# Copying x inside DRAM in 5 KB pieces, and three dummy products that read a constant of the preamble

## The chip, the cores and the metric

The kernel runs on one core of one Trainium2 chip. The metric is the device time of one execution in microseconds (us); smaller is better. Three runs of the kernel before gave 662.64, 663.84 and 665.05 us, so its median is 663.84 us.

## The reference

The kernel computes one transformer layer with its two branches in parallel, for a sequence of 2048 rows of width 640 in bf16. Cut to what matters:

```python
B, S, D, H = 1, 2048, 640, 32          # Dh = 20; F = 1536
xn = _layernorm(x)                     # per row
q = (xn @ wq).reshape(B, S, H, Dh)     # 32 heads of queries
k = xn @ wk                            # ONE head of keys, shared by all
v = xn @ wv                            # ONE head of values
p = softmax(q @ k.T * Dh ** -0.5)      # 32 x 2048 x 2048 scores
A = (p @ v) @ wo
h = relu(xn @ w1 + b1)
B = (h * h) @ w2 + b2
return x + A + B
```

## The kernel before

**Stages.** The rows of x are loaded in 16 tiles of 128 rows (`X0` to `X12`, L622, on the queues of SyncE and ScalarE). Each tile is normalised: `bn_stats` and `bn_aggr` on VectorE (L662 to L664) or two activations on ScalarE (L657, L658), a reciprocal root on ScalarE (first four tiles) or as a power on GpSimd (`PW4` to `PW15`, L676), and the product (`XN..`, L677) on VectorE or GpSimd. TensorE transposes the tile (`T..`, L700), VectorE or ScalarE evacuates it into `xnT` (`TE..`, L694, L696). From `xnT` come the keys (`K..`, `KT..`), the queries (`Q0_..`, `Q1`, `QC..`) and the values (`V..`, L703).

**The long middle.** For 32 blocks of 512 query rows by 4 heads, TensorE makes score tiles of 128 keys by 512 queries (`q:` and `d:` in the order). ScalarE takes the exponential of two of them at a time (L1083); part of the tiles goes to VectorE (L1093), GpSimd (L1106) and accumulating transfers instead, which build the exponential from four shifted copies in 16-bit arithmetic. TensorE then multiplies by the values (`v:`, `u:`). The feed-forward branch (`FFN..`, `FP..`, `OUT..`) and the query projections of later blocks are woven in between. L600 is the one line of nearly all matmuls.

**The order.** Each engine follows a list written out by hand (`ORDER`), in program order. An operation waits by semaphores for what it depends on; if it waits, everything behind it on its engine waits too. Three stretches of these lists matter here.

- TensorE begins with `W4 W5 W6`, three 128x512 dummy products into banks 4, 5 and 6 (L710), then thirteen more (`warm:`, L1041). Seven of those wait for nothing but the two constants, six for steps of the row statistics. Then come `T0 T1 T2 T3 K0 Q0_0 ...`. Later stands `q:38,39 q:40,41 Q1 Q1 T12 Q1 T13 q:42,43 Q1 q:44,45 Q1 KT6`.
- GpSimd runs `... PW11 XN11 PW12 XA PW13 PW14 XN14 PW15 XN15 LIB` and then the shifted copies.
- SyncE issues `X0 X2 wq0 X4 X6 X8 b2 X12 xb b1 w11 wq w10 w20 w22 w23 w13 QD2_2 ...`. Some of these hold until a named step: `xb` and `wq` wait for `TE2`, `b1` for `TE5`.

**The steps that the change touches.** `W4 W5 W6` multiply `ones_bf` (128x128) by `hT_tmp[:, 0, :]` (128x512 zeros). Both are set by VectorE (`ones`, L604, and `zero`, L605), and the three products wait for them. `xb` is a copy of x from its input in DRAM to a scratch tensor in DRAM (L647), 2560 KB, whose two sides are written as 128 rows of 20 KB. GpSimd's `XA` (L648) waits for it, and adds the bias b2 to it in DRAM; from there `XR..` (L869) fetches x + b2 tile by tile, from 53 us on, for the residual (L890, L900). `wq` (L628) brings the query weights apart from the first 80 columns; `Q1` (L773) and all `QC..` need it. `BC..` (L969) spreads the reciprocals of the softmax sums over the rows of the heads: its source has the heads as outermost dimension, one to four of them.

```python
nc.const_aps.tensor(1.0, (128, n), BF16)   # in the changed kernel: a bf16 constant of one column,
                                           # set by GpSimd before the engines start, read as n columns
```

Of the kernel before, what the change touches and what calls it, by code (L numbers as in the profile page):

```python
# [7 lines left out]
BF16 = mybir.dt.bfloat16  # L8
# [30 lines left out]
def _pl(z):  # L39
# [20 lines left out]
HOLD = dict(wq="TE2", b1="TE5", w1=("TE4", "TE6", "TE8", "TE10"), w2=("TE12", "TE13", "TE14", "TE15"), wo=("RL3_2", "RL3_4"), wd="RL3_7",  # L60
            fr=[f"OUT{16 + k}.16" for k in range(4)])
# [433 lines left out]
def bass_parallel_sum__grouped_kv_mqa__dense_activation_squared_relu__prompt_kernel(nc, A_x, A_wq, A_wk, A_wv, A_wo, B_x, B_w1, B_b1, B_w2, B_b2, out):  # L495
    es = ExitStack()
    with es:
        def sb(name, shape, dt):
            return es.enter_context(nc.sbuf_tensor(name, list(shape), dt))
# [28 lines left out]
        ones_bf = OR[:, 1, 0:64].bitcast(BF16)  # L528
# [7 lines left out]
        hT_tmp = sb("hT_tmp", [128, 2, 512], BF16)  # L536
# [8 lines left out]
        ps = es.enter_context(nc.psum_tensor("ps", [128, 8, 512], F32))  # L545
# [23 lines left out]
        xb = nc.dram_tensor("xb", [S, D], BF16, kind="Internal").ap()  # L569
# [14 lines left out]
        def one():  # L584
            nsem[0] += 1
            return newctr(f"d{nsem[0]}")
# [3 lines left out]
        def op(name, eng, fn, deps=(), **kw):  # L590
            o = Op(name, eng, fn if isinstance(fn, list) else [fn], deps, **kw)
            assert name not in made, name
            made[name] = o
            return o

        def load(name, eng, fn, deps=()):
            return op(name, eng, fn, deps, dma=one())
# [6 lines left out]
        c_ones = op("ones", "DVE", lambda e: e.memset(ones_bf[:], 1.0))  # L604
        c_zero = op("zero", "DVE", lambda e: e.memset(hT_tmp[:, 0, :], 0.0))  # L605
# [38 lines left out]
            lambda e: e.dma_start(wd32[:, DH:32, 1, :], hrows(wr0)[:, 8:DH, :])))]  # L644
        op("texp", "ACT", lambda e: e.preload_act_table_set("natural_log_exp_and_others"))
        l_b2 = load("b2", "SP", lambda e: e.dma_start(b2r[0].rearrange("(a n) -> a n", a=ST), B_b2.rearrange("(o n) -> o n", o=1).to_broadcast([ST, D])))
        l_xb = load("xb", "SP", lambda e: e.dma_start(xb.rearrange("(p a) d -> p (a d)", p=128), A_x[0].rearrange("(p a) d -> p (a d)", p=128)), [HOLD["wq"]])  # L647
        xa_op = op("XA", "POOL", lambda e: e.dma_start(xb.rearrange("(p a) d -> p (a d)", p=128).rearrange("p (k n) -> p k n", k=5),  # L648
                                                       b2r.rearrange("o (k n) -> o k n", k=5).to_broadcast([128, 5, 2048]), accum_op=ALU.add, max_dma_last_dim=4096), [l_b2, l_xb], dma=one())

# [55 lines left out]

        VB0, WB = SHARED[2], 7
        k_of, q_of, v_of, vs_of, first_rel = {}, {b: [] for b in range(NBLK)}, {}, {}, {}
        for bk in SHARED:
            op(f"W{bk}", "PE", lambda e, bk=bk: e.matmul(ps[:, bk, :], ones_bf[:, :], hT_tmp[:, 0, :], start=True, stop=True), [c_ones, c_zero])  # L710
        vmm = []
        for st in range(4):
            cs = slice(128 * st, 128 * st + 128)
# [316 lines left out]
        for e in ENG:  # L1030
            nth = {}
            for word in ORDER[e].split():
                w, _, ns = word.partition("@")
                ns = [int(x) for x in ns.split(",")] if ns else []
                k, _, a = w.partition(":")
# [52 lines left out]
        for _, a, e, ns in planned("e"):  # L1088
            u, hs = int(a.split(".")[0]), [int(h) for h in a.split(".")[1]]
            x = sets.setdefault(u, Terms())  # L1090
            i, n = len(x.order), len(hs)
# [8 lines left out]
        for u, x in sets.items():  # L1100
            assert sorted(x.order) == list(range(HPG))
            for j in range(1, NTERM):
                w = f"{u}.{j}"
                if ("p", w) in plan:
                    e, ns = plan["p", w]
# [3 lines left out]
                elif ("j", w) in plan:  # L1109
                    e, ns = plan["j", w]  # L1110
# [210 lines left out]
```

## Time and profile before

| | us |
|---|---|
| three runs | 662.64, 663.84, 665.05 |
| median | 663.84 |
| profiled execution | 664.51 |
| its span, first to last instruction | 662.7 |
| busy in it: TensorE, ScalarE, VectorE, GpSimd | 654.4, 649.7, 625.3, 536.7 |

The profile is of one execution. The difference between 664.51 and 662.7, 1.8 us, lies before the first and behind the last instruction. In the views a row gives a start (us from the span's start), a duration, an engine (PE is TensorE's matmuls, PEld its weight loads, DVE VectorE, ACT ScalarE, POOL GpSimd, SP SyncE; SPq and POOLq are the engines' DMA queues), the line, the operation with out<-in, the count, and in brackets the idle time before it with what ended it. The DMA view gives packets, bytes, and the share of the time of 16 DMA engines that they took.

### The profile page before, as it was taken

The page shows a single profiled execution, that of the slowest core. Times are in us where ns is not written, and L with a number is a line of the kernel's source. Part 1 is how long each engine was busy: PE and PEld are TensorE (multiplying, and loading weights), DVE is VectorE, ACT ScalarE, POOL GpSimd, SP SyncE. Part 2 cuts the span into 40 slices and gives each one's busy share as a digit, 9 for nine tenths or more (in the row PEclk, how much of TensorE's full clock was granted, in tenths as well). Part 3 has the DMA queues.
Part 4 walks back from the last instruction along what each step waited for, and adds up shares of the span by engine and source line. Part 5 has one row for each costly group of instructions (what it writes and reads, how often), then busy time and mean ns, then how long its engine had stood idle before and what let it go on. Part 6 is the DMA issues. An engine that isn't in the chain of part 4 may idle for free.

```text
span 662.7 us, 22005 instructions
## 1 busy us (share of the span) xinstructions
PE 654.4 (99%) x9422; PEld 216.9 (33%) x9422; DVE 625.3 (94%) x1123; ACT 649.7 (98%) x716; POOL 536.7 (81%) x532
## 2 busy tenths in 40 slices
PE   8999999999999999999999999999999999999998
PEld 4432222333322223333332222333333322223444
DVE  8879999999999999999999999999999999999997
ACT  7999999999999999999999999999999999999996
POOL 1729899899898889898999989888999988899400
PEclk9999999999999999999999999999999999999999
DMA  8794857888897995696957645798888654858732
GB/s 293 187 245 96 185 110 163 166 183 187 185 186 161 183 182 120 129 184 125 178 107 155 122 92 99 151 189 170 158 174 165 132 121 91 178 105 177 141 110 71
DMA packets 53814, 102.06 MB, mean 154 GB/s; under 512 B 15948, under 2 KB 31452, under 8 KB 53652
## 3 DMA queue, kind: packets, MB, share of 16 engines
q0 software_dynamic: 18544, 68.17, 55.4%
q1 hardware_dynamic: 34308, 31.94, 16.8%
q8 instruction: 74, 1.21, 0.8%
q10 hardware_dynamic: 864, 0.54, 0.3%
q14 instruction: 24, 0.20, 0.1%
HBM read 23.26 MB, written 10.01 MB: 50 GB/s over the span
## 4 chain that ended last, share of the span: by engine, by line
PE 58%; ACT 34%; DMA 3%; DVE 3%; SPq 1%; issue 0%; POOL 0%
PE ps L600 57%; ACT PT L1083 34%; DVE tx L1093 1%; DMA tx<-tx 1%; DMA cmore<-drs 1%; DMA tx<-in_A_x_dram 1%; PE ps L1005 1%; SPq L800 0%; SPq L969 0%; SPq L963 0%; DVE xnT L694 0%; SPq L622 0%; DVE OR L662 0%; PE ps L700 0%; PE ps L703 0%
## 5 line engine op out<-in xcount | busy, mean ns | idle before, releaser
L1083 ACT ACTIVATE PT<-ps 128x1024 bf16<-128x1024 f32 (+1 forms) x693 | 640.4, 1089 | 2.3 <-PE ps L600 1.9
L1093 DVE TENSOR_SCALAR tx<-ps 128x512 uint16<-128x512 f32 x656 | 424.8, 683 | 21.8 <-PE ps L600 15.1
L1106 POOL INT64_ADD tx<-tx x375 | 396.3, 1132 | 54.3 <-DVE big L836 15.2
L600 PE MATMUL ps<-qT,kT 20*128 20x512 bf16 x2048 | 265.4, 384 | 3.3 <-ACT PT L1083 1.2
L600 PEld LDWEIGHTS ps<-qT,kT 20*128 20x128 bf16 x2048 | 69.0, 91 | 248.7 <-ACT PT L1083 132.4
L600 PE MATMUL ps<-PT,vx 128*32 128x512 bf16 x1392 | 131.7, 383 | 0.0
L1130 POOL DMA_DIRECT2D tx<-tx x118 | 121.3, 1028 | 10.3 <-POOL tx L1106 7.8
L600 PE MATMUL ps<-tx,vxs 128*32 128x512 bf16 x1220 | 115.4, 384 | 0.0
L600 PE MATMUL ps<-tx,vx 128*32 128x512 bf16 x864 | 81.3, 384 | 0.5 <-DMA tx<-tx 0.5
L600 PE MATMUL ps<-w_sb,big 128*32 128x320 bf16 x1536 | 79.1, 302 | 0.0
L600 PE MATMUL ps<-xnT,w_sb 128*32 128x512 bf16 x960 | 78.0, 383 | 0.0
L1107 DVE TENSOR_SCALAR tx<-tx 128x2048 uint16<-128x2048 uint16 x89 | 61.2, 700 | 0.6 <-PE ps L600 0.2
L600 PEld LDWEIGHTS ps<-PT,vx 128*32 128x32 bf16 x1392 | 34.6, 95 | 39.1 <-issue 31.1
L600 PEld LDWEIGHTS ps<-w_sb,big 128*32 128x32 bf16 x1536 | 33.8, 95 | 30.2 <-issue 20.0
L600 PEld LDWEIGHTS ps<-tx,vxs 128*32 128x32 bf16 x1220 | 30.0, 94 | 36.1 <-issue 27.1
L828 DVE TENSOR_SCALAR hT_tmp<-ps,b1col 128x512 bf16<-128x512 f32 x48 | 35.7, 744 | 0.8 <-PE ps L600 0.6
L600 PE MATMUL ps<-xnT,wq_sb 128*32 128x512 bf16 (+2 forms) x480 | 35.5, 357 | 0.0
L600 PEld LDWEIGHTS ps<-tx,vx 128*32 128x32 bf16 x864 | 21.4, 94 | 26.2 <-issue 21.5
L600 PEld LDWEIGHTS ps<-xnT,w_sb 128*32 128x32 bf16 x960 | 19.9, 95 | 28.8 <-issue 19.3
L600 PE MATMUL ps<-wo_c,OC 128*32 128x320 bf16 x496 | 28.0, 301 | 0.0
L1112 POOL INT64_ADD tx<-tx x14 | 26.9, 1924 | 0.9 <-DVE big L836 0.5
L944 DVE COPY OR<-ps 128x512 f32<-128x512 f32 x30 | 20.4, 680 | 1.7 <-PE ps L600 1.6
(87 smaller groups left out, 221.5 us busy)
## 6 DMA issues: line engine op xcount, KB each, us to landing
tx<-tx POOLq DMA_DIRECT2D x111, 512.0 KB, 5.9
tx<-tx POOLq DMA_DIRECT2D x7, 1024.0 KB, 8.8
w_sb<-in_B_w_dram SPq DMA_DIRECT2D x8, 480.0 KB, 9.6
big<-OR SPq DMA_DIRECT2D x71, 40.0 KB
xb<-in_A_x_dram SPq DMA_DIRECT2D x1, 2560.0 KB, 11.1
xb<-b2r POOLq DMA_DIRECT2D x1, 2560.0 KB, 19.8
xr<-xb SPq DMA_DIRECT2D x16, 160.0 KB, 3.2
out_dram<-out_sb SPq DMA_DIRECT2D x14, 160.0 KB, 3.6
```

The lines of the kernel that those rows point to most:

```text
L600: return lambda e: e.matmul(out_(), l, val(r), start=val(start), stop=val(stop), tile_position=tp, skip_group_check=loose)
L828: o = evac(ref, f"RL{qc}_{f}", "DVE", lambda e: e.tensor_scalar(out=hT_tmp[:, k % 2, :], in0=ps[:, ref.n, :], scalar1=b1col[:, f:f + 1], s ...
L944: tn = evac(pv_ref[b], f"TN{b}", "DVE", lambda e: e.tensor_copy(out=OR[:, a, :], in_=acc()), or_users[a])
L1005: parts = [lambda e, l=l, r=r, first=first, last=last: e.matmul(ps[:, at(ref), 0:HW], l, r, start=first, stop=last, skip_group_check=k < N ...
L1083: o = op(f"a:{a}", e, lambda e, qk=qk, slots=slots: e.activation(out=some(PT, slots), in_=some(ps, [r.n for r in qk.takes]), func=AF.Exp, ...
L1093: o = op(f"e:{a}", e, lambda e, x=x, i=i, n=n, refs=refs: e.tensor_scalar(out=x.ref(0)[:, i * 512:(i + n) * 512].bitcast(U16) if n == 1 el ...
L1106: fn = dict(POOL=lambda e, x=x, j=j: e.int64_add(out=x.ref(j).bitcast(I64), in0=x.ref(0).bitcast(I64), in1=TSTEP * j * 0x0001000100010001) ...
L1107: DVE=lambda e, x=x, j=j: e.tensor_scalar(out=x.ref(j).bitcast(U16), in0=x.ref(0).bitcast(U16), scalar1=TSTEP * j, scalar2=None, op0=ALU.a ...
L1112: o = op(f"j:{w}", e, lambda e, x=x: e.int64_add(out=two(*sorted((x.at[2], x.at[3]))).bitcast(I64), in0=two(*sorted((x.at[0], x.at[1]))).b ...
L1130: fn = (lambda e, x=x: e.dma_start(*reversed(sums_of(x.at)), accum_op=ALU.add)) if k == "b" else (lambda e, x=x, p=pairs[0]: e.dma_start(x ...
```

## The change

Two edits. The copy `xb` names the same bytes on both sides in another order: four groups outermost, 128 rows in each, and 4 rows of x (5 KB) as the contiguous piece. The three products `W4 W5 W6` read the preamble's constant of ones for both operands and no longer wait for VectorE's two memsets; their results are not used by anything.

```diff
-        l_xb = load("xb", "SP", lambda e: e.dma_start(xb.rearrange("(p a) d -> p (a d)", p=128), A_x[0].rearrange("(p a) d -> p (a d)", p=128)), [HOLD["wq"]])
+        l_xb = load("xb", "SP", lambda e: e.dma_start(xb.rearrange("(p g a) d -> g p (a d)", p=128, g=4), A_x[0].rearrange("(p g a) d -> g p (a d)", p=128, g=4)), [HOLD["wq"]])
...
+        def ones(n):
+            return nc.const_aps.tensor(1.0, (128, n), BF16)
+
         for bk in SHARED:
-            op(f"W{bk}", "PE", lambda e, bk=bk: e.matmul(ps[:, bk, :], ones_bf[:, :], hT_tmp[:, 0, :], start=True, stop=True), [c_ones, c_zero])
+            op(f"W{bk}", "PE", lambda e, bk=bk: e.matmul(ps[:, bk, :], ones(128), ones(512), start=True, stop=True))
```

## The prediction

> **What bounds the kernel now.** I read the page first, then the busy time by stretch, then the timeline of the first 45 us, then the DMA view of the stretches around the copy.
>
> ```profile
> span 662.7 us, 22005 instructions
> PE 654.4 (99%) x9422; PEld 216.9 (33%) x9422; DVE 625.3 (94%) x1123; ACT 649.7 (98%) x716; POOL 536.7 (81%) x532
> 30.00:40.00 10.00, 9.80 (x159) 4.50 (x157) 6.48 (x18) 9.93 (x12) 2.70 (x4) 1.00 1.05 210
> 200.00:600.00 400.00, 399.32 (x5592) 122.67 (x5592) 383.07 (x647) 399.37 (x436) 360.64 (x350) 1.00 0.73 145
> 27.45 33.51 ACT L1083 ACTIVATE PT<-ps 128x1024 bf16<-128x1024 f32 x36
> ```
>
> In the rows of stretches the columns after the length are the busy time of PE, PEld, DVE, ACT and POOL. From 200 to 600 us PE idles for 0.7 us and ACT for 0.6 us; at 27.45 us begins a run of 36 exponentials without a gap. So both engines are full, and what stops both of them early in the kernel is not made good later: it is added to the end. A gain must shorten the start, and a loss only has to break that chain once.
>
> **The three products.** They start after VectorE's memsets and are followed by the other dummies.
>
> ```profile
> 0.82 0.17 DVE L604 MEMSET OR<- 128x128 bf16 x1 [0.82 <-PEq L1306]
> 1.31 1.46 PE L710 MATMUL ps<-hT_tmp,OR 128*128 128x512 bf16 x3 [1.31 <-DVE PT L608]
> 2.57 4.60 PE L1041 MATMUL ps<-hT_tmp,OR 128*128 128x512 bf16 x13
> 5.55 1.61 PE L1041 MATMUL ps<-hT_tmp,OR 128*128 128x512 bf16 x6
> 7.25 1.39 PEld L700 LDWEIGHTS ps<-ident,big 128*128 128x128 bf16 x20 [0.58 <-DVE big L677]
> ```
>
> Without the wait they can start when VectorE could, at 0.82 instead of 1.31 us, so the row of dummies moves up by 0.5 us. Its end doesn't matter as such: the transposes at 7.25 us wait 0.58 us for VectorE's normalised rows (L677), which no dummy product holds up, and the last dummies wait for VectorE's statistics. I cost it at 0. The bounds: the first real products could find TensorE in a better or worse state. The 20 transposes after 7.25 us have 1.39 us of weight loads; were they half as fast, that would cost 1.4 us, and I know of nothing that would gain more than the 0.5 us of the move. Reading one column 512 times is not in this trace; if it made a product longer, 7.25 − 0.82 = 6.4 us for sixteen products is the cover. I keep −0.5 to +1.4 us for the range.
>
> **The copy: how many DMA engines carry it.** This is the step that decides.
>
> ```profile
> xb<-in_A_x_dram SPq DMA_DIRECT2D x1, 2560.0 KB, 11.1
> 9.80 0.50 SPq L647 DMA_DIRECT2D xb<-in_A_x_dram  x1
> DMA packets 94, 2.33 MB, mean 284 GB/s; under 512 B 30, under 2 KB 36, under 8 KB 36
> q1 hardware_dynamic: 92, 2.30, 81.2%
> ...
> DMA packets 27, 0.00 MB, mean 3 GB/s; under 512 B 27, under 2 KB 27, under 8 KB 27
> ...
> 639.08 0.64 SPq L969 DMA_DIRECT2D big<-drs  x1
> DMA packets 84, 0.16 MB, mean 80 GB/s; under 512 B 6, under 2 KB 6, under 8 KB 84
> q1 hardware_dynamic: 84, 0.16, 21.1%
> ```
>
> The third and fourth lines are the DMA view of 11.2 to 19.4 us, where the copy now runs (the next line, 18.6 to 19.5 us, has no large packet left): 58 packets over 8 KB hold nearly all 2.3 MB, some 40 KB each, so the 128 contiguous rows are joined and cut anew, and the queue takes 81% of 16 engines. The last two are the same view of 640.6 to 642.6 us, when one transfer (issued at 639.08) is alone on the queue: L969, whose source has four heads as its outermost dimension. Its 78 packets of 2 KB take 21% of 16 engines, close to 4/16, at 80 GB/s. So a transfer with four groups outermost is carried by four engines. The changed copy has four groups outermost on both sides, and in that order its pieces are not contiguous, so they can't be joined again. I take four engines.
>
> The Trainium skill states the rule on the page "DMA: Bandwidth & Descriptors", section "Why a DMA increments its semaphore by 16 and not by 1": a transfer runs on the largest number of engines up to 16 that divides the slowest dimension of both patterns, on this queue the lowest-numbered ones. By that rule 128 gives 16 and 4 gives 4; the two rows above agree. With the page's 27 GiB/s for each engine the moved time would be an estimated 22.6 us, 5 us less than the one below.
>
> The time: 0.16 MB in 2 us at 21.1% of 16 engines is 80/(0.211 × 16) = 23.7 GB/s for each busy engine. The copy's 2.62 MB over four engines is then 2.62/(4 × 23.7) = 27.7 us. The copy's own row gives 284 × (2.30/2.33)/(0.812 × 16) = 21.6 GB/s with all engines in each other's way, 30.4 us; larger pieces than 2 KB could save some 5% (an estimate), 26.4 us. I take 27.7. Landing minus moving is now 11.1 − 8.2 = 2.9 us (0.5 to issue, some 0.9 to the first byte at 11.2, 1.5 to the signal). So the bytes end at 11.2 + 27.7 = 38.9 us and the copy lands at 40.4 instead of 20.9 us.
>
> **Who waits.** What SyncE issues behind the copy has a share on every engine, and a queue seems to be served in order: `b1`, issued at 16.06 in the rows below, 12 pieces of 256 B, is among the 27 small packets of 18.6 to 19.5 us above, when the copy is through.
>
> ```profile
> 16.06 0.40 SPq L631 DMA_DIRECT2D b1row<-in_B_b_dram  x1
> 19.09 0.60 SPq L630 DMA_DIRECT2D w_sb<-in_B_w_dram  x1
> 19.73 0.64 SPq L628 DMA_DIRECT2D wq_sb<-in_A_wq_dram  x1
> wq_sb<-in_A_wq_dram SPq DMA_DIRECT2D x1, 700.0 KB, 5.7
> DMA packets 1387, 1.27 MB, mean 372 GB/s; under 512 B 32, under 2 KB 1387, under 8 KB 1387
> 29.29 0.61 PE L600 MATMUL ps<-xnT,wq_sb 128*20 128x512 bf16 x8
> ```
>
> The fifth line is the DMA view of 21.5 to 24.9 us. `w11` (480 KB) and `wq` (700 KB), 1.21 MB, take 3.25 us at 372 GB/s; on the four engines their shares begin only at 38.9, end at 42.15, and the signal comes 0.5 us later (now 25.4 against 24.9): 42.65 us. `Q1` on PE uses `wq` at 29.29 us without a wait. It would start 13.4 us late, and everything behind it on PE.
>
> ```profile
> 25.96 1.82 POOL L648 DMA_DIRECT2D xb<-b2r  x1
> 27.99 0.56 POOL L676 TENSOR_TENSOR rstd<-mv,nhalf 128x1 f32<-128x1 f32 x1 [0.21 <-DVE mv L667]
> 29.00 0.75 DVE L677 TENSOR_SCALAR big<-tx,mv,rstd 128x640 bf16<-128x640 bf16 x2
> 30.56 0.47 PE L700 MATMUL ps<-ident,big 128*128 128x128 bf16 x5
> ```
>
> The second chain: `XA` on GpSimd, now issued at 25.96 with the copy landed 5 us before, would wait until 40.4. Behind it on GpSimd stand `PW13`, `PW14`, `XN14`, `PW15`, `XN15`. `PW13` ends at 40.4 + 1.82 + 0.56 = 42.8; VectorE, held at `XN13` (the second half of its row at 29.00), is done 0.4 us later, and T13 on PE starts at 43.2 instead of 30.56: 12.6 us late. The two chains nearly tie; `wq` is the later. TensorE has given out scores for about two exponentials when it stops, so ScalarE runs dry some 2 us behind it and restarts as far behind: the whole 13.4 us reach the end.
>
> To that comes a restart of TensorE after a long idle time. At the kernel's start the first three dummies take 1.46 us, 0.49 each, the last six, from 5.55 us on (a part of the row of thirteen above), 1.61 us, 0.27 each. So TensorE is at about half speed for the first 5.55 − 1.31 = 4.2 us of its work. Bounds: 0 (it stays fast, or ScalarE hides it), or half of 4.2, 2.1. I take 1.5, nearer to the upper end, since both engines are full there. On the page "TensorE: Matmul & The Clock Gate" (Part 1) the Trainium skill says that the clock halves after an idle window of 3.4 us and returns after a busy one; by it the cost would be an estimated 1.7 us.
>
> The sum: 664.5 + 0 (products) + 13.4 + 1.5 = 679.4 us for an execution like the profiled one. That one lies 0.7 us above the median of the three runs, so the forecast is 678.7 us. With the copy's ends alone it is 677.4 to 681.4; with those of the restart and of the products as well, 675.4 to 683.4, say 676 to 683.
>
> **Rivals.** *Not slower: the copy is spread over 16 engines.* If the pieces are dealt out one by one whatever the outermost dimension is, the copy lands near 20.9 us as now, XA has its 5 us of slack, `wq` is in time, and the time is 664 us, within 0.3%, which is 2 us, about what a measurement of this kernel can tell from no change. It decides at once: any copy that lands before 25.9 us and lets `wq` land before 29.3 costs nothing. Against it is the row of L969; for it, that that row is of a broadcast into SBUF, not of a copy within DRAM. Chance 0.13. That the pieces are joined again, so that the change isn't there, ends at the same time and is in that chance.
>
> *Much slower: the addition catches up with the weights.* GpSimd's addition then works on the same four engines.
>
> ```profile
> w_sb<-in_B_w_dram SPq DMA_DIRECT2D x4, 480.0 KB, 13.5
> q0 software_dynamic: 595, 2.44, 89.6%
> q1 hardware_dynamic: 344, 0.44, 10.8%
> ```
>
> That is 28.6 to 43 us, the time of XA: it takes 90% of the engines, 16 × 14.4/595 = 0.39 us for each packet, and the loads beside it land after 13.5 us. Its first packets come about 2.6 us after its issue, so at 43.0, when `wq`'s last bytes are due at 42.15. If the loads slip by over 0.9 us, each piece of `wq` left on an engine waits for a packet of the addition; with half of the 40 pieces left that is 20 × 0.39 = 8 us, so 686 us. Chance 0.22.
>
> *Faster by over 0.3%* would need 2 us from the first 13 us, where the products give 0.5 at most, or an unseen gain of twelve free engines. Chance 0.03.
>
> **The numbers.** Forecast 678.7 us, 0.56 for 676 to 683; 0.06 for less than that, down to 673, if the pieces move faster than any row here shows. The range 673 to 687 takes in these and the caught-up addition at 686, about 0.8, and leaves out the case of no change. Faster 0.03, same 0.13, slower 0.84.
>
> **What would show it.** Right: in the DMA view the copy at about a quarter of 16 engines, 512 packets more of under 8 KB, landing some 30 us after its issue; PE idle for about 13 us before `Q1` (L600 with wq_sb) with a DMA as what ended it, ACT idle as long, XA's start on POOL near 40 us; the rest of the span as before. Wrong: a landing near 11 us, or PE without a gap at 30 us. If the gap is there and ends with XN13's transpose, the chain over GpSimd was the later one. A start of L710 near 0.8 us with T0 still at 7.25 us would show the products' cover.

## The result, and the profile after

The changed kernel takes 679.75 us (median of four runs, 679.07 to 680.6) against 663.91 us for the kernel before (four runs beside it, 662.64 to 665.05). The ratio is 1.0238 (95% interval 1.0219 to 1.0257): slower by 2.4%. The forecast was 678.7 us. Ratios here and below leave out disturbed runs of either kernel, so one may differ a little from the quotient of the medians.

The lines of the code behind the edit have moved by three: L710 is now L713, L1041 is L1044, L1083 is L1086. First the page of the kernel after: span, busy time, the clock granted to TensorE in 40 slices of 16.9 us, and packets.

```profile
span 677.6 us, 22005 instructions
...
PE 659.3 (97%) x9422; PEld 217.8 (32%) x9422; DVE 625.6 (92%) x1123; ACT 649.6 (96%) x716; POOL 536.7 (79%) x532
...
PEclk9959999999999999999999999999999999999999
...
DMA packets 54250, 102.06 MB, mean 151 GB/s; under 512 B 15936, under 2 KB 31440, under 8 KB 54152
```

ScalarE did the same 649.6 us of work in a span that is 14.9 us longer. Something slow shows only in the third slice of the clock. Where the 14.9 us went is read from ScalarE's busy time by stretch (length, busy time and instructions, clock, DMA share, GB/s), the kernel before first:

```profile
30.00:45.00 15.00, 14.93 (x17) 1.00 1.05 227
45.00:60.00 15.00, 15.00 (x18) 1.00 0.48 140
60.00:100.00 40.00, 40.00 (x45) 1.00 0.71 144
100.00:200.00 100.00, 98.87 (x108) 1.00 0.85 179
200.00:600.00 400.00, 399.37 (x436) 1.00 0.73 145
```

The same stretches of the kernel after:

```profile
30.00:45.00 15.00, 1.89 (x3) 0.61 0.72 186
45.00:60.00 15.00, 11.95 (x13) 0.71 1.04 255
60.00:100.00 40.00, 40.00 (x45) 1.00 0.57 123
100.00:200.00 100.00, 99.73 (x109) 1.00 0.81 168
200.00:600.00 400.00, 399.72 (x436) 1.00 0.74 147
```

Between 30 and 60 us ScalarE loses 29.93 − 13.84 = 16.1 us. From 60 us on it loses nothing more, and it takes back 0.86 + 0.35 = 1.2 us, since the few gaps that it had between 100 and 600 us nearly close. 16.1 − 1.2 = 14.9 us: the account is complete, and the loss lies in two stretches of 15 us. Some 0.3 of the 1.2 us is not the change's doing: from 200 to 600 us ScalarE is busy for 399.6 to 399.7 us in the kernels of experiments 2 to 4 too, in which nothing or nearly nothing stops.

What happens there is in the timelines of the kernel after (start, duration, engine, line, operation, count, and in brackets the idle time before with what ended it). TensorE first, then GpSimd and SyncE's queue, each a view by itself:

```profile
0.76 1.44 PE L713 MATMUL ps<-const-bfloat16-1.0 128*128 128x512 bf16 x3 [0.76 <-PEq L1309]
...
7.21 0.96 PE L700 MATMUL ps<-ident,big 128*128 128x128 bf16 x11
...
29.08 0.40 PE L600 MATMUL ps<-qT,kT 20*128 20x512 bf16 x4
41.08 1.03 PE L600 MATMUL ps<-xnT,wq_sb 128*20 128x512 bf16 x8 [11.60 <-DVE mv L670]
...
43.24 0.73 PE L700 MATMUL ps<-ident,big 128*128 128x128 bf16 x5
```

```profile
25.54 0.55 POOL L676 TENSOR_TENSOR rstd<-mv,nhalf 128x1 f32<-128x1 f32 x1
37.89 1.82 POOL L648 DMA_DIRECT2D xb<-b2r  x1 [11.80 <-DMA xb<-in_A_x_dram]
```

```profile
9.76 0.74 SPq L647 DMA_DIRECT2D xb<-in_A_x_dram  x1
16.32 5.55 SPq L631 DMA_DIRECT2D b1row<-in_B_b_dram  x1
21.91 0.62 SPq L630 DMA_DIRECT2D w_sb<-in_B_w_dram  x1
22.57 7.00 SPq L628 DMA_DIRECT2D wq_sb<-in_A_wq_dram  x1
```

The products start at 0.76 us, and T0 still starts at 7.21. TensorE stands still before `Q1`, for 11.60 us; GpSimd stands still before `XA`, for 11.80 us. Behind the copy even SyncE is held: issuing `b1` takes 5.55 us (0.40 before), issuing `wq` 7.00 us (0.64 before). The DMA view of 11.2 to 19.4 us, the stretch that the prediction showed of before, has the reason, and the same view of 11.2 to 37 us the landing of `wq`:

```profile
q1 hardware_dynamic: 168, 0.80, 25.8%
```

```profile
GB/s 81 81 79 103 103 137 103 100 103 103 95 119 103 95 119 103 103 112 131 147 244 369 239 96 111 111 103 103 111 112 185 274 391 371 135 103 103 111 141 210
...
wq_sb<-in_A_wq_dram SPq DMA_DIRECT2D x1, 700.0 KB, 18.4
```

Four of sixteen engines carry the copy (25.8%, where 81.2% were busy before), at 103 GB/s in most slices; the peaks come some 2 to 3 us behind the issues of weights at 21.91 and 29.61 us, so I read them as the weights' shares on the twelve other engines. `wq` lands at 22.57 + 18.4 = 40.97 us.

One line must be read with care. The bracket of `Q1` names `mv L670`, a small VectorE step that ended at 40.94 us, and the chain of waits that the profile follows back goes the same way, through 27.82 us of the copy:

```profile
9.76 27.82 DMA xb<-in_A_x_dram
37.58 0.31 issue
37.89 1.82 POOL xb L648
39.71 0.63 POOL rstd L676
40.36 0.45 DVE big L677
41.08 1.03 PE ps L600 x6
```

So the view blames the chain over GpSimd, though `wq` lands 0.03 us behind that step and `Q1` reads `wq`. With two causes this close a releaser that is inferred can't decide; experiments 5 and 6 do.

### The profile page after: what moved, and what is told of

Its sections match the earlier page's. It is cut to its first block, busy times and chain, and to the rows that moved or that the text cites. A ratio compares the mean times of both kernels' runs of the same rounds, so it can differ in the third digit from the quotient of the medians.

```text
span 677.6 us, 22005 instructions
## 1 busy us (share of the span) xinstructions
PE 659.3 (97%) x9422; PEld 217.8 (32%) x9422; DVE 625.6 (92%) x1123; ACT 649.6 (96%) x716; POOL 536.7 (79%) x532
## 2 busy tenths in 40 slices
DMA packets 54250, 102.06 MB, mean 151 GB/s; under 512 B 15936, under 2 KB 31440, under 8 KB 54152
## 4 chain that ended last, share of the span: by engine, by line
PE 61%; ACT 31%; DMA 4%; DVE 2%; POOL 0%; issue 0%; DVEq 0%
PE ps L600 60%; ACT PT L1086 31%; DMA xb<-in_A_x_dram 4%; DVE tx L1096 1%; PE ps L1008 1%; PE ps L700 0%; POOL xb L648 0%; ACT xnT L696 0%; DVE OR L662 0%; DVE OR L663 0%; DVE ident L613 0%; DVE OC L893 0%; DVE PT L1020 0%; DVE PT L611 0%; DVE big L677 0%
## 5 line engine op out<-in xcount | busy, mean ns | idle before, releaser
L1086 ACT ACTIVATE PT<-ps 128x1024 bf16<-128x1024 f32 (+1 forms) x693 | 640.2, 1090 | 16.9 <-PE ps L600 16.7
L1133 POOL DMA_DIRECT2D tx<-tx x118 | 121.4, 1029 | 10.3 <-POOL tx L1109 7.8
```

Of the source, the lines that this page charges most:

```text
L1086: o = op(f"a:{a}", e, lambda e, qk=qk, slots=slots: e.activation(out=some(PT, slots), in_=some(ps, [r.n for r in qk.takes]), func=AF.Exp, ...
L1133: fn = (lambda e, x=x: e.dma_start(*reversed(sums_of(x.at)), accum_op=ALU.add)) if k == "b" else (lambda e, x=x, p=pairs[0]: e.dma_start(x ...
```

## The experiments

The theory: the copy's outermost dimension puts it on four engines; two chains behind it, `wq` to `Q1` and `XA` to T13, each stop TensorE for some 12 us; the restart at half clock adds the rest; the products cost nothing. The rivals: the piece of 5 KB or the order of the bytes is what is slow; only one chain matters, so that moving one step repairs the kernel; the clock's part is small or is not the clock. The kernel before had medians of 663.68, 663.75 and 664.57 us beside the three groups of runs (1 to 4, 5 to 8, 9 to 11).

**1. The copy alone.** The kernel after with the old products.

```diff
-            op(f"W{bk}", "PE", ... ones(128), ones(512), start=True, stop=True))
+            op(f"W{bk}", "PE", ... ones_bf[:, :], hT_tmp[:, 0, :], start=True, stop=True), [c_ones, c_zero])
```

> The kernel before with the changed copy alone; the three products as they were. Theory (the copy on four engines is all of the loss): the time of the changed kernel, 679.8 us, within 1.5. Rival (the products on the constant cost or gain something of their own): off from 679.8 by what the products are worth, over 1.5 us. The copy's bytes should again end near 37 us, the dot product of query weights and rows (Q1) start near 41 us.

Measured: 680.48 us (679.34 to 681.06), ratio 1.0247 (1.0214 to 1.0279); `XA` is issued at 38.02 us and `Q1` starts at 41.21. The copy is the whole loss.

**2. The products alone.** The kernel after with the old copy.

```diff
-        l_xb = ... "(p g a) d -> g p (a d)", p=128, g=4 ...
+        l_xb = ... "(p a) d -> p (a d)", p=128 ...
```

> The kernel before with the three products on the constant of ones alone; the copy as it was. Theory: the products start 0.55 us earlier (0.76 instead of 1.31 us) and the transposes still start at 7.2 us, since VectorE's rows hold them up: 663.9 us, no change within 0.3%. Rival (an earlier start shortens the span): 663.4 us or less, with the transposes before 7.0 us.

Measured: median 663.7 us of twelve executions, ratio 1.0015 (0.9979 to 1.0051). Eleven took 662.22 to 670.4 us, as did the kernel before beside it (662.22 to 670.88), and one 1075.95. In the profile the products start at 0.76 us, T0 at 7.20, `Q1` at 28.88. No difference that this measurement can tell: the 6.4 us of cover hold.

**3. Sixteen groups outermost, the pieces still 5 KB.** The kernel after with another split.

```diff
-        l_xb = ... "(p g a) d -> g p (a d)", p=128, g=4 ...
+        l_xb = ... "(p g a) d -> g p (a d)", p=32, g=16 ...
```

> The changed kernel with the same 512 pieces of 5 KB, but 16 groups of 32 outermost instead of 4 of 128. Theory (the outermost count sets how many DMA engines carry the copy): 16 engines, the copy is through by about 19 us as before the change, no gap on TensorE at 29 us, 663.9 us within 0.3%. Rival (pieces of 5 KB that step through DRAM are slow by themselves): the copy takes 26 us or more again and the time stays near 680 us.

Measured: 663.39 us (662.44 to 668.04), ratio 1.0011 (0.9989 to 1.0032). The DMA view of 11.2 to 19.4 us, GpSimd's and TensorE's timelines of this kernel:

```profile
q1 hardware_dynamic: 495, 2.46, 94.5%
```

```profile
25.61 1.82 POOL L648 DMA_DIRECT2D xb<-b2r  x1
```

```profile
28.94 0.61 PE L600 MATMUL ps<-xnT,wq_sb 128*20 128x512 bf16 x8
```

The same 512 pieces of 5 KB, now on 94.5% of the engines, and neither chain waits. The size of the piece costs nothing; the number of groups outermost does. It gains nothing either: this kernel and the one before can't be told apart.

**4. Eight groups outermost.** To find where the slack ends.

```diff
-        l_xb = ... "(p g a) d -> g p (a d)", p=128, g=4 ...
+        l_xb = ... "(p g a) d -> g p (a d)", p=64, g=8 ...
```

> The changed kernel with 8 groups of 64 outermost. Theory: 8 engines, so half of four engines' 26 us, 13 us: the bytes end near 24.3 us and the copy lands near 25.2, just before GpSimd's addition is due at 25.96; the query weights behind it end 3.3 us later and land near 28, before Q1 at 29.3. So nothing waits: 664 us within 0.5%. Rival (the loss grows in proportion to the time that the copy takes): 13 us of copying more than at 16 engines would cost about half of what 4 engines cost, some 670 us.

Measured: 663.9 us (663.08 to 664.71), ratio 0.9985 (0.9957 to 1.0014). GpSimd's and TensorE's timelines:

```profile
26.04 1.82 POOL L648 DMA_DIRECT2D xb<-b2r  x1 [0.34 <-DMA xb<-in_A_x_dram]
```

```profile
29.94 0.61 PE L600 MATMUL ps<-xnT,wq_sb 128*20 128x512 bf16 x8 [0.85 <-DMA wq_sb<-in_A_wq_dram]
```

Both chains just begin to wait, 0.34 and 0.85 us, and here the profile names the two DMAs. Two waits of under 1 us are within the noise of the total. Eight engines are the edge of the slack.

**5. `wq` ahead of the copy on SyncE.** This frees the `wq` chain alone.

```diff
-        "X0 X2 wq0 X4 X6 X8 b2 X12 xb b1 w11 wq w10 ...
+        "X0 X2 wq0 X4 X6 X8 b2 X12 wq xb b1 w11 w10 ...
```

> The changed kernel (copy on four engines) with SyncE issuing the query weights wq ahead of the copy instead of behind it. Theory (two chains, the weights by 1 to 2 us the later): Q1 is no longer late, but GpSimd's addition still waits for the copy until about 40 us (the copy starts some 2 us later), so VectorE stops at XN13 and TensorE at T13, near 42 us instead of 30.6: about 11 to 12 us lost and a slow restart, 678 to 681 us, little change. Rival (the weights are the only chain): 664 to 667 us.

Measured: 678.8 us (three runs from 678.27 to 679.17, one of 688.98), ratio 1.0229 (1.0208 to 1.0251), as expected of two chains that tie. TensorE's and GpSimd's timelines:

```profile
28.80 0.61 PE L600 MATMUL ps<-xnT,wq_sb 128*20 128x512 bf16 x8
...
42.89 0.73 PE L700 MATMUL ps<-ident,big 128*128 128x128 bf16 x5 [12.75 <-DVE mv L667]
```

```profile
39.91 1.82 POOL L648 DMA_DIRECT2D xb<-b2r  x1 [14.43 <-DMA xb<-in_A_x_dram]
```

`Q1` runs at 28.80 us, while the L670 step that the bracket blamed comes only at 42.81 us here: so `Q1` doesn't need that step, and in the kernel after it was `wq` that it waited for. TensorE now stops a few instructions later, at T13, for the chain over GpSimd, and the kernel loses nearly as much. A part of this stop is the experiment's own: with `wq` ahead of it the copy lands later, and `XA` is issued 2.0 us later than in the kernel after. There T13 could have started near 37.89 + (42.89 − 39.91) = 40.9 us, still 10.3 us late.

**6. `XA` behind GpSimd's rows.** This frees the other chain alone.

```diff
-        ... PW11 XN11 PW12 XA PW13 PW14 XN14 PW15 XN15 LIB p:27.1@2 ...
+        ... PW11 XN11 PW12 PW13 PW14 XN14 PW15 XN15 LIB XA p:27.1@2 ...
```

> The changed kernel with GpSimd's addition of the bias moved behind the last row statistics (behind XN15 and LIB), so that no row waits for the copy; wq stays behind the copy on its queue. Theory: Q1 still waits for wq until about 41 us: 679 to 680 us, no change. Rival (GpSimd's chain sets the time): 664 to 668 us.

Measured: 680.97 and 682.23 us in the two runs with a mean granted clock near 0.985 (ratio 1.0274, 1.0245 to 1.0304); two more, with a mean clock of 0.958, took 695.68 and 696.97. The profile is of the last of these. TensorE's timeline:

```profile
41.28 1.03 PE L600 MATMUL ps<-xnT,wq_sb 128*20 128x512 bf16 x8 [11.67 <-DMA wq_sb<-in_A_wq_dram]
```

With GpSimd free `Q1` still waits, 11.67 us, and the profile now names `wq`. Experiments 5 and 6 together show two chains of nearly one length. `XA` is issued only at 51.17 us here, and in this execution TensorE stops a second time, 2.23 us up to 72.76 us, for a transfer of queries; whether the two shorter executions had that stop is not known.

**7. Both moved.** If these two chains were all, the time would be that of the kernel before.

```diff
-        ... PW12 XA PW13 PW14 XN14 PW15 XN15 LIB ...
+        ... PW12 PW13 PW14 XN14 PW15 XN15 LIB XA ...
...
-        ... X12 xb b1 w11 wq w10 ...
+        ... X12 wq xb b1 w11 w10 ...
```

> The changed kernel with both edits of the two runs beside it: wq ahead of the copy and the addition behind the rows. Theory (two chains and no third): no gap on TensorE near 30 us; the copy on four engines is hidden and lands near 40 us, the addition near 59 us, some 6 us after the first fetch of its sum is due on SyncE at 53 us, which may cost little or nothing: 664 to 668 us. Rival (the four loaded engines hold up something else too, for instance the weights w1 and w2 behind the copy): over 670 us.

Measured: the gap at 30 us is gone (`Q1` at 28.98 us), but twelve runs spread from 664.37 to 688.0 us; the eight up to 673.13 give a ratio of 1.0054 (1.0006 to 1.0103). Four lie in the theory's range of 664 to 668, seven above the 670 of the rival. They follow the granted clock: 664.4 to 665.4 at 1.000, 668.8 to 672.6 at 0.992, 688.0 at 0.968. (Eight of 29 executions of the kernel before, too, took 666.5 to 670.9 us at 0.990 to 0.997.) The one profile is of an execution of 686.45 us, a span of 684.6. It shows a third wait on TensorE, and the DMA view of 45 to 60 us what is beside it:

```profile
61.80 0.62 PE L600 MATMUL ps<-qT,kT 20*128 20x512 bf16 x4 [7.25 <-DMA qT<-QCr]
```

```profile
q0 software_dynamic: 629, 2.53, 86.0%
q1 hardware_dynamic: 945, 0.74, 17.4%
```

A transfer of queries, 20 KB or less, stands beside the addition (q0, 86% of the engines, some 16 us later than in the kernel before) and the weights that were held up behind the copy. So in this execution the late copy reaches a third place, which the kernel after doesn't show, perhaps because TensorE's other waits come first. That the executions of 664 us lack this wait is inferred from their clock of 1.000; none of them was profiled. The best runs reach the time of the kernel before; none beats it.

**8. Dummy products in the wait, 32 groups.** To hold the clock while TensorE waits; the extra products add zeros to a sum.

```diff
-        ... q:38,39@3,4 q:40,41@5,6 Q1@2 ...
+        ... q:38,39@3,4 q:40,41@5,6 fill (32 times) Q1@2 ...
```

> The changed kernel with 32 groups of dummy products (zeros added to a sum that is already there) ahead of Q1, so that TensorE works through most of the wait. Theory (after the wait TensorE runs at half its clock for over 10 us and ScalarE starves, some 3 us): the granted clock stays at 1.00 between 30 and 60 us, and the time falls by 2 to 3.5 us to about 677 us. Rival (the slow restart is hidden by ScalarE's own queue): 679.8 us as before, whatever the clock.

Measured: 679.5 us, ratio 1.0239 (1.0215 to 1.0262), no change. TensorE's timeline and the stretch of 41 to 53.8 us (TensorE's busy time, clock):

```profile
29.23 7.09 PE L600 MATMUL ps<-kT,zeros 128*32 128x512 bf16 x128
41.70 1.04 PE L600 MATMUL ps<-xnT,wq_sb 128*20 128x512 bf16 x8 [5.37 <-DVE mv L670]
```

```profile
41.00:53.80 12.80, 11.91 (x141) 0.66 1.05 205
```

The 128 products took only 7.09 us, so 5.37 us of idle time were left before `Q1`, and the clock fell all the same: some 8 us at half clock behind `Q1`, which itself starts 0.6 us later than in the kernel after. So this is no test of what a held clock is worth. It is a control for experiment 10, which holds it: dummy products that lose the clock gain nothing.

**9. Three moved.** Experiment 7, and the weights `w20 w22 w23` and two fetches of x + b2 moved behind the transfers of queries that came too late there.

```diff
-        ... b1 w11 wq w10 w20 w22 w23 w13 QD2_2 ... QD3_1 OM0_1 SL0 XR12 ... XR14 ... QD5_1 ...
+        ... wq xb b1 w11 w10 w13 QD2_2 ... QD3_1 w20 w22 w23 OM0_1 SL0 ... QD5_1 XR12 XR14 ...
```

> The changed kernel with wq ahead of the copy and the addition behind the rows, as in the run both_moved, and in addition three of the four loads of w2 issued behind the query pieces of the next blocks instead of ahead of them, and the first two fetches of x + b2 issued some 20 us later. Theory (in both_moved TensorE stops near 54 us because the query pieces wait on the loaded engines behind the weights and beside the addition): no gap on TensorE near 54 us, the granted clock 1.00 throughout, 664 to 666 us and a narrow spread. Rival (the addition alone holds the query pieces up): a gap of several us near 55 us remains and the times spread from 664 to 688 us as before.

Measured: 670.42 to 683.7 us in four runs, with mean clocks from 0.995 to 0.975; ratio 1.0128 (1.0054 to 1.0203). The expectation failed. TensorE's timeline and the waits of 40 to 80 us:

```profile
69.64 0.61 PE L600 MATMUL ps<-qT,kT 20*128 20x512 bf16 x3 [5.20 <-DVE tx L1096]
```

```profile
DVE R L950 <- DMA R<-drs: 5.5, 1, 5.5
```

The wait near 54 us is gone and another has taken its place: the next small transfer, `R<-drs` of 8 KB, lands 10.9 us after its issue; in the kernel before it landed after 1.9. In SyncE's order the weights that I moved away from the one transfer now stand shortly before the other, and from 58 to 64 us its queue takes 69 to 107% of the engines; from 64 to 68 us GpSimd's accumulating transfers take over 100%, the addition of b2 being through by then. VectorE waits 5.5 us for it, and TensorE 5.2 us for VectorE. Which order would free all of these small transfers stays open.

**10. Dummy products in the wait, 52 groups.**

```diff
-        ... q:38,39@3,4 q:40,41@5,6 Q1@2 ...
+        ... q:38,39@3,4 q:40,41@5,6 fill (52 times) Q1@2 ...
```

> The changed kernel with 52 instead of 32 groups of dummy products ahead of Q1, since 32 took only 7.1 of the 12.5 us of the wait and left TensorE idle for 5.4 us, after which the clock fell all the same. Theory (the half clock after the wait costs about 3 us): with TensorE busy to within 1 us of the weights' landing the granted clock stays at 1.00 from 30 to 60 us and the time falls to 676 to 677.5 us. Rival (ScalarE's queue hides it): 679.5 us.

Measured: 674.8 us (674.6 to 674.99), ratio 1.0151 (1.0115 to 1.0187). TensorE's timeline, and the stretch of 41 to 53.8 us (TensorE's busy time, clock):

```profile
28.92 11.41 PE L600 MATMUL ps<-kT,zeros 128*32 128x512 bf16 x208
41.33 0.61 PE L600 MATMUL ps<-xnT,wq_sb 128*20 128x512 bf16 x8 [1.01 <-DVE mv L670]
```

```profile
41.00:53.80 12.80, 12.21 (x189) 1.00 1.01 205
```

The same stretch of the kernel after:

```profile
41.00:53.80 12.80, 12.72 (x134) 0.50 1.03 207
```

`Q1` starts as late as in the kernel after (41.33 against 41.08), yet the kernel is 679.75 − 674.8 = 4.9 us faster (4.8 by the spans, 677.6 and 672.8; the intervals of the two ratios don't overlap). What differs behind the wait is the clock. The kernel after runs at half clock for 12.7 us behind the wait and does 134 matmuls in this stretch where this one does 189. Not all of the 4.9 us need be the clock's: ScalarE's loss between 30 and 60 us falls from 16.1 to 12.4 us (busy for 17.52 us there instead of 13.84), by 3.7, and the rest of the difference lies in stretches where the two kernels do the same, half a microsecond of it before the wait. So the half clock costs 3.7 to 4.9 us, more than the 2 to 3.5 that were expected.

**11. Two groups outermost.** The other end of the row of 16, 8 and 4.

```diff
-        l_xb = ... "(p g a) d -> g p (a d)", p=128, g=4 ...
+        l_xb = ... "(p g a) d -> g p (a d)", p=256, g=2 ...
```

> The changed kernel with 2 groups of 256 outermost. Theory (the outermost count is the number of engines, each moves a piece of 5 KB in about 0.2 us): 256 pieces for each engine, 52 us, the bytes end near 63 us, the weights behind them near 67 us, Q1 some 38 us late: 702 to 708 us, more if the clock stays low for longer. Rival (a limit other than the engines sets 26 us): near 680 us.

Measured: 703.25 us (702.97 and 703.52), ratio 1.0579 (1.0521 to 1.0638). GpSimd's timeline and SyncE's queue:

```profile
62.12 1.82 POOL L648 DMA_DIRECT2D xb<-b2r  x1 [36.70 <-DMA xb<-in_A_x_dram]
```

```profile
15.64 30.44 SPq L631 DMA_DIRECT2D b1row<-in_B_b_dram  x1
```

TensorE's timeline, where its clock comes back (eight products in 1.05 us, then four in 0.40):

```profile
71.86 1.05 PE L600 MATMUL ps<-PT,vx 128*32 128x512 bf16 x8
72.84 0.40 PE L600 MATMUL ps<-qT,kT 20*128 20x512 bf16 x4
```

From `Q1` on TensorE does the same steps as in the kernel after, yet its half clock ends some 7.5 us behind the start of `Q1`, not 12.7.

The four runs in one table:

| groups outermost | share of 16 engines, 11.2 to 19.4 us | `XA` issued | `Q1` | time |
|---|---|---|---|---|
| 16 | 94.5% | 25.61 | 28.94 | 663.39 |
| 8 | 49.9% | 26.04 | 29.94 | 663.9 |
| 4 | 25.8% | 37.89 | 41.08 | 679.75 |
| 2 | 12.9% | 62.12 | 65.28 | 703.25 |

The share is the number of groups over sixteen. From 4 to 2 groups `XA` is issued 24.2 us later, and `Q1` starts 24.2 us later.

## Why the prediction was right

**The products, 0 us: right.** They start 0.55 us earlier and T0 doesn't move. Experiment 2 bounds them at −0.2 to +0.5%; reading one column 512 times takes 1.44 us for three products, against 1.46.

**Four engines: right, and shown.** The row of L969, a broadcast into SBUF, was good evidence for a copy within DRAM. The table gives the rule for 16, 8, 4 and 2, and experiment 3 clears the size of the piece. The rule that the prediction cited from the Trainium skill ("DMA: Bandwidth & Descriptors", section "Why a DMA increments its semaphore by 16 and not by 1") agrees with all four rows. Packets of under 8 KB rose from 53652 to 54152, by 500; 512 were forecast, and some records can be missing.

**The copy's time: 2.8 us too long.** I took 23.7 GB/s for each engine, from pieces of 2 KB. The slices show 103 GB/s on four engines, 25.8 GB/s each, so 2.62 MB take 25.4 us, under the lower bound of 26.4, for which I had guessed a saving of 5% without a row. The bytes end near 37 us (the first slices are slower) instead of 38.9, and by the chain the copy lands at 37.58 instead of 40.4: the signal came within 1 us of the bytes, not 1.5. By the 27 GiB/s (29 GB/s) for an engine that the Trainium skill gives ("DMA: Bandwidth & Descriptors", section "Specifications") the moving would take an estimated 22.6 us; the measured rate lies between that figure and my row.

**Two chains that nearly tie, `wq` the later: right, and shown** by experiments 5 and 6; `wq` is the later by some 0.1 us (40.97 against the 40.9 us at which T13 could have started). Sizes: `wq` landed at 40.97 us (42.65 forecast) and `Q1` started at 41.08, so it is 41.08 − 29.29 = 11.8 us late where I had 13.4.

**The restart: the step that was mis-sized.** I took 1.5 us and bounded it by 2.1, from the 4.2 us for which a dummy product takes 0.49 instead of 0.27 us at the kernel's start. That is read from durations; the clock row shows 1.00 there. Behind the wait the row shows 0.50 for 12.7 us, and that cost 3.7 to 4.9. What the prediction quoted of the Trainium skill ("TensorE: Matmul & The Clock Gate", Part 1, full clock again after a busy window of 3.4 us) disagrees with this row too: by the profile TensorE was busy for 12.72 of the 12.80 us of the stretch. The work differs: at the start dummies of 128 x 128 by 512, here tiles with 20 or 32 rows or columns, and transposes. That can't be the whole reason: in experiment 11 the same steps behind the wait ran at half clock for 7.5 us only. What decides its length stays open.

**The sum came out right with two errors in it.** Forecast against the profiled execution: 13.4 + 1.5 = 14.9 us; measured by the spans: 14.9. The parts, by the spans: with the clock held (experiment 10) the wait alone costs 672.8 − 662.7 = 10.1 us, and the half clock adds 4.8 (3.7 by ScalarE's stretch of 30 to 60 us). Against 13.4, the wait was 1.6 us shorter, ScalarE made up to 1.2 us good in gaps that it had later, where I said nothing would be, and half a microsecond is not accounted for; the clock cost 2.2 to 3.4 more than my 1.5. That the two errors cancel is luck: a forecast within 1.1 us of the result here is no proof of its terms.

**The rivals.** Sixteen engines: ruled out by the share. The addition that catches up with the weights, 686 us: it did not happen in the kernel after. `wq` landed at 40.97 us, and the addition, issued at 37.89 with first packets some 2.6 us later, hardly met it. Experiments 7 and 9 show something like it one step on: `R<-drs`, 8 KB, lands after 6.7 and 10.9 us there, 1.9 in the kernel before, beside the addition in the one, behind weights and beside GpSimd's other accumulating transfers in the other. The times there reach 688.0 and 683.7 us. That each piece waits for a packet of the addition was not shown.

## What to carry to other kernels

Before a copy is split anew, count what stands outermost: a copy within DRAM can lose three quarters of its engines by a change of order that moves the same bytes, and the piece size can be had with 16 groups outermost as well. Then list what is queued behind it on every queue and engine: here one transfer off the critical path held a weight load, a chain of rows and, with both of these freed, a row of small transfers, so that moving one step alone gave nothing back. And price a stop of TensorE with more than its length, and as a range: the half clock behind it lasted 5.5 to 12.7 us in experiments 5, 8 and 11 and in the kernel after.

## What the runs showed of the hardware that was not expected

- A transfer on few engines can also hold the engine that issues: SyncE's issue of the 3 KB `b1` took 0.40 us behind the old copy, 0.36 us behind the one on eight engines, 5.55 us behind the one on four and 30.44 us behind the one on two.
- The half clock behind a wait does not follow the wait's length. It lasted 5.5 us behind 12.75 us of idle time (experiment 5), 7.5 behind 36.48 (experiment 11), 8 behind 5.37 (experiment 8) and 12.7 behind 11.60 (the kernel after). In the profiled execution of experiment 7 a wait of 7.25 us was followed by a clock of 0.50 from 60 to 80 us and 0.54 from 80 to 100 us, though TensorE was busy for the whole of the second stretch (busy time of PE, PEld, DVE, ACT and POOL behind the length, then the clock, DMA share and GB/s). What decides how long it lasts stays open.

```profile
80.00:100.00 20.00, 20.00 (x160) 3.90 (x163) 12.55 (x20) 13.11 (x13) 10.84 (x12) 0.54 0.48 108
```

- 208 dummy products with 32 output columns, 11.41 us of them, kept the clock at 1.00 through the wait; 128 of them with 5.37 us of idle time behind did not.
